# State products and scores in 64x64 tiles of TensorE, one PSUM bank of outputs per head, low parts of nine pairs by GpSimd

## The chip, the cores and the metric

The kernel runs on one core of a Trainium2 chip. The metric is the device time of one execution in microseconds (us), and the median of three runs before the change is 563.88 us (563.80 to 564.11). The core has five engines that each work through a list of instructions in order: TensorE (PE, matmuls, with its weight loads shown as PEld), VectorE (DVE), ScalarE (ACT), GpSimd (POOL), and SyncE (SP), which issues the DMAs. They wait for one another on semaphores.

## The reference

Four batches, eight heads of width 64 and 768 positions go through a linear attention with decay, in blocks of 64, and its output is the input of a mixer with two dense layers over positions and two over channels:

```python
for b in range(nb):                     # blocks of 64 positions
    intra = (qb @ kb.T * Dmask) @ vb    # Dmask[i,j] = lam**(i-j) for i >= j
    inter = (qb * lam**(pos+1)) @ kv_state
    out[:, :, sl] = intra + inter
    kv_state = lam**block * kv_state + (kb * lam**(block-1-pos)).T @ vb
x = out as (batch, 768, 512)
u = x + (relu(x.T @ w_tok1) @ w_tok2).T
result = u + relu(u @ w_ch1) @ w_ch2
```

All of it is in fp32.

## The kernel before, in words

The sixteen pairs of heads (batch b, two heads of 64 each) are the unit of the attention. Blocks of 128 positions are used, so a pair has six blocks c = 0 to 5. Head h of a pair lies in partitions h*64 to h*64+63 of the transposed q and k (`qT`, `kT`).

The main loop (L641 to L725) is written out by hand: the order in which the code calls the engines is the order of each engine's list. I call its pass with index i "turn i". Turn i makes the scores of pair i+1, the outputs of pair i and the state products of pair i+1, turns (transposes) q and k of pair i+2, issues the loads of v of pair i+3 and of q and k of pair i+4, and turns the outputs of pair i back. Beside that it takes `work`, up to five groups of the mixer's token layers (`token_hidden`, 18 matmuls of 256 columns; `token_out`, 6 matmuls of 384 columns) from a queue; turns 0 to 3 have none, turns 4, 5, 6, 11 and 12 have two, turns 7 and 10 five, 8, 9 and 13 four, 14 three and 15 one. `cuts` says how many groups stand ahead of the first `turn_back`, between the two and behind the second. `later` hands out pieces of the conversion of the weights (the `narrow` steps, mostly on DVE, and `split`, on ACT and POOL) between them.

What a turn does for the attention:

- `scores` (L290): for each of two halves g of three blocks, and each head, one matmul of K = 64 rows, M = 128 weight columns, N = 128 (shown as tile 64*128), each head in a PSUM bank of its own; then DVE multiplies by the decay mask into `a` (L307).
- `scale_q` (L249): POOL multiplies q by the powers of lam into `qs` (L252).
- `state` (L258): ten matmuls (tile 128*64, N = 64) make the state contributions `kv` in a bank, a scan on DVE (L273) sums them over the blocks into `sv`, and `place` copies them on POOL (L286) to `stb`, a block-diagonal 128x128 matrix for each block: head h's 64x64 state in the rows and columns of head h, zeros elsewhere. Two `stb` buffers are cleared at the start (L189).
- `outputs` (L315), twice: for three blocks each, two matmuls of the weights `a` with v (L323, K = 128, M = 64) and two of `stb` with `qs` (L333, K = 128, of which half the rows are zeros) into one bank `xT`, head h in partitions h*64 on; then ACT copies the bank to `uT` (L340).
- `turn_q` (L223): q of pair i+2 from pair 5 on, and k from pair 8 on, are loaded in pieces such that DVE's 32x32 transposes finish the turn (L226, L229); the earlier pairs are turned by PE through PSUM (`turn_k` L216, `turn_q_rows` L236) and copied by ACT.
- `turn_back` (L344), twice: PE turns three blocks of `uT` into a bank `xp` (L355), ACT rounds them to `xhi` (L363) and DVE makes the low parts `xlo` = xp - xhi (L364). Both feed `token_hidden`.

An fp32 matmul shows as two MATMUL records in the trace, a transpose or one in fp32r (the mixer's) as one.

PSUM has eight banks: four for `sc` (two buffers of two banks), one named `xT`, and three that rotate under the tag `sh`, which serve `kv`, the second output half, `kt`, `qt`, `xp` and the mixer's groups in the order of the calls. A tile of `sh` waits until the tile three places before it has been read.

After turn 15 the remaining token layers and the sixteen units of the channel layers follow (about two thirds of the time); the change does not touch their code.

Of the kernel before, what the change touches and what calls it, by code (L numbers as in the profile page):

```python
# [22 lines left out]
def kernel(  # L23
# [199 lines left out]
    def turn_q(i):  # L223
        qTs[i] = kp.tile([P, S], F32, tag="qT", bufs=2, name=f"qT{i}")
        if i >= NQ:
            nc.vector.transpose(out=qTs[i], in_=loaded[i][1])  # L226
        if i >= NKD:
            kTs[i] = kp.tile([P, S], F32, tag="kT", bufs=2, name=f"kT{i}")
            nc.vector.transpose(out=kTs[i], in_=krs[i])  # L229
# [28 lines left out]
    def state(i):  # L258
# [22 lines left out]
        st = stb[i % 2]  # L281

        def place():
            for h in range(2):
                r = slice(h * D, (h + 1) * D)
                nc.gpsimd.tensor_copy(out=st[r, :, h, :], in_=sv[r].rearrange("p (e c) -> p c e", c=NC - 1))  # L286

        return place

    def scores(i):  # L290
        b, p = pairs[i]
        for g in range(2):
            pair = two_banks(f"sc{i}{g}", 3 * P)
            sc = [pair[:, h] for h in range(2)]
            for c in range(3):
                cs = slice((3 * g + c) * P, (3 * g + c + 1) * P)
                for h in range(2):
                    r = slice(h * D, (h + 1) * D)
                    nc.tensor.matmul(  # L299
                        out=sc[h][:, c * P : (c + 1) * P],  # L300
                        lhsT=kTs[i][r, cs],
                        rhs=qTs[i][r, cs],
                        start=True,
                        stop=True,
                    )
# [9 lines left out]
    def outputs(i, g):  # L315
        b, p = pairs[i]
        st = stb[i % 2]
        xT = bank("sh" if g else "xT", f"xT{i}{g}", 3 * P)
        for cg in range(3):
            c = 3 * g + cg  # L320
            cs = slice(cg * P, (cg + 1) * P)
            for h in range(2):
                nc.tensor.matmul(  # L323
                    out=xT[h * D : (h + 1) * D, cs],
                    lhsT=vns[i][:, h, c, :],
                    rhs=weights_of[i, g, h][:, cg, :],
                    start=(cg == 0),
                    stop=False,
                )
            if c == 0:  # L330
                continue
            for h in range(2):
                nc.tensor.matmul(  # L333
                    out=xT[h * D : (h + 1) * D, cs],
                    lhsT=st[:, c - 1, h, :],
                    rhs=qss[i][:, c - 1, :],
                    start=False,
                    stop=(cg == 2),
                )
        nc.scalar.copy(out=uT[b][:, p, 3 * g * P : (3 * g + 3) * P], in_=xT)  # L340
# [300 lines left out]
    for i in range(-2, NI):  # L641
# [668 lines left out]
```

## Time and profile before

| What | us |
|---|---|
| runs (median, lowest, highest) | 563.88, 563.80, 564.11 |
| the profiled execution | 563.57 |
| its span, first to last instruction | 561.6 |
| around the span | 2.0 |
| PE busy in the span | 544.1 |
| DVE busy | 433.4 |
| POOL busy | 271.6 |
| ACT busy | 244.2 |
| scores of pair 1 begin (turn 0) | 13.86 |
| scores of pair 8 begin (turn 7) | 75.70 |
| scores of pair 15 begin (turn 14) | 151.35 |
| outputs of pair 15 end (turn 15) | about 166 |
| one group of `token_hidden` on PE (turn 14, 160.06 to 162.18) | 2.1 |
| one group of `token_out` on PE (turn 15, 163.42 to 164.67, with two changes of tile shape) | 1.2 |

The first group of numbers is of the whole execution, the rest of the stage that the change touches. A turn lasts 6.6 to 7.5 us without groups of the mixer and 9.7 to 12.4 us with them.

### The profile page before, as it was taken

What the parts mean: (1) busy time and instruction counts of PE and PEld (TensorE: products, weight loads), DVE (VectorE), ACT (ScalarE), POOL (GpSimd) and SP (SyncE); (2) the same over time, 40 slices, a digit from 0 to 9 for tenths busy, and PEclk for the clock granted to TensorE, in tenths of its full rate; (3) what the DMA queues carried; (4) which work ended last, traced back from release to release, by engine and by line L of the source; (5) the groups of instructions that cost most, each with busy time, mean ns of one, the idle gap of its engine ahead of it and who ended that gap; (6) DMA issues with size and microseconds to landing.
All of it is one profiled execution on the core that took longest, in us unless ns stands there. A gap on an engine that the chain in (4) does not pass through costs nothing.

```text
span 561.6 us, 10781 instructions
## 1 busy us (share of the span) xinstructions
PE 544.1 (97%) x4186; PEld 529.2 (94%) x4186; DVE 433.4 (77%) x650; ACT 244.2 (43%) x490; POOL 271.6 (48%) x248
## 2 busy tenths in 40 slices
PE   5999998999999999999999999999999999999994
PEld 4888887999999999999999999999999999999994
DVE  4786789598787989887878887888678777785683
ACT  3564442336253554343444344353455545442421
POOL 5666452557214464443444454453466656662330
PEclk9999999999999999999999999999999999999998
DMA  9998999999102433351725300015864131320337
GB/s 185 253 205 198 211 166 182 188 190 155 28 2 82 176 119 131 104 215 40 246 73 210 109 1 1 0 29 75 212 113 136 57 114 57 113 76 0 45 49 133
DMA packets 176019, 65.72 MB, mean 117 GB/s; under 512 B 163552, under 2 KB 166752, under 8 KB 175968
## 3 DMA queue, kind: packets, MB, share of 16 engines
q1 hardware_dynamic: 172224, 63.75, 47.8%
q10 hardware_dynamic: 3744, 1.28, 0.9%
q8 instruction: 33, 0.54, 0.4%
q14 instruction: 18, 0.15, 0.1%
HBM read 48.24 MB, written 16.78 MB: 116 GB/s over the span
## 4 chain that ended last, share of the span: by engine, by line
PE 82%; DVE 6%; SPq 5%; DMA 4%; ACT 1%; issue 1%; DVEq 0%; ACTq 0%
PE po L1007 23%; PE pa L794 12%; PE pc L794 9%; PE pb L794 7%; PE pa L981 6%; PE pc L981 5%; PE ph L451 4%; PE pd L794 3%; SPq L111 3%; PE sc L299 2%; PE xT L323 2%; DMA vn<-in_v_dram 2%; PE pu L488 2%; PE pu L471 1%; PE xT L333 1%
## 5 line engine op out<-in xcount | busy, mean ns | idle before, releaser
L1022 DVE TENSOR_TENSOR uT<-po,uT 128x768 f32<-128x768 f32 x62 | 58.9, 952 | 22.6 <-PE po L1007 22.3
L286 POOL COPY stb<-sv 64x320 f32<-64x320 f32 x32 | 26.8, 838 | 45.0 <-DVE sv L273 44.1
L805 ACT ACTIVATE c<-c 128x384 f32<-128x384 f32 x42 | 22.1, 526 | 59.2 <-DVE c L850 33.4
L987 DVE TENSOR_TENSOR uT<-pa,uT 128x768 f32<-128x768 f32 x32 | 30.6, 956 | 11.0 <-PE pa L981 10.3
L323 PE MATMUL xT<-a,vn 128*64 128x128 f32 x384 | 35.7, 277 | 0.0
L340 ACT COPY uT<-xT 128x384 f32<-128x384 f32 x32 | 15.3, 478 | 46.2 <-PE xT L333 46.2
L807 POOL TENSOR_TENSOR h22l<-c,h22h 128x384 fp32r<-128x384 f32 x14 | 14.4, 1030 | 41.6 <-ACT h22h L806 41.6
L307 DVE TENSOR_TENSOR a<-sc,mask 128x768 f32<-128x768 f32 x32 | 29.0, 948 | 5.1 <-PE sc L299 5.1
L333 PE MATMUL xT<-qs,stb 128*64 128x128 f32 x320 | 31.3, 273 | 0.0
L987 DVE TENSOR_TENSOR uT<-pc,uT 128x768 f32<-128x768 f32 x24 | 22.9, 955 | 10.6 <-PE pc L981 10.6
L375 POOL TENSOR_TENSOR c1l<-cs,c1h 128x512 fp32r<-128x512 f32 x15 | 19.2, 1292 | 23.2 <-ACT c1h L374 23.2
L451 PE MATMUL ph<-xhi,w1h 128*128 128x256 f32 x96 | 28.2, 294 | 1.3 <-DVE sv L273 0.9
L1007 PE MATMUL po<-h12h,c 128*128 128x384 f32 x112 | 28.7, 337 | 0.0
L1007 PE MATMUL po<-h11h,c 128*128 128x384 f32 x112 | 28.6, 336 | 0.0
L1007 PE MATMUL po<-h21h,c 128*128 128x384 f32 x112 | 28.6, 336 | 0.0
L1007 PE MATMUL po<-h22h,c 128*128 128x384 f32 x112 | 28.6, 336 | 0.0
L451 PE MATMUL ph<-xhi,w1l 128*128 128x256 f32 x96 | 27.1, 282 | 0.0
L451 PE MATMUL ph<-xlo,w1h 128*128 128x256 f32 x96 | 27.1, 282 | 0.0
L299 PE MATMUL sc<-qT,kT 64*128 64x128 f32 x384 | 26.4, 285 | 0.2 <-ACT qT L237 0.2
L299 PEld LDWEIGHTS sc<-qT,kT 64*128 64x128 f32 x384 | 23.4, 192 | 3.3 <-issue 1.8
L364 DVE TENSOR_TENSOR xlo<-xp,xhi 128x384 fp32r<-128x384 f32 x32 | 17.6, 552 | 11.2 <-ACT xhi L363 11.0
L252 POOL TENSOR_TENSOR qs<-qT,lamp 128x640 f32<-128x640 f32 x16 | 25.2, 1577 | 0.3
(401 smaller groups left out, 1928.8 us busy)
## 6 DMA issues: line engine op xcount, KB each, us to landing
raw<-in_moe_w_ch_dram SPq DMA_DIRECT2D x20, 512.0 KB, 3.8
vn<-in_v_dram SPq DMA_DIRECT2D x16, 384.0 KB, 5.2
kn<-in_k_dram SPq DMA_DIRECT2D x30, 192.0 KB, 5.4
out_dram<-y SPq DMA_DIRECT2D x96, 48.0 KB, 1.9
qn<-in_q_dram SPq DMA_DIRECT2D x44, 96.0 KB, 3.9
kr<-in_k_dram SPq DMA_DIRECT2D x32, 96.0 KB, 2.8
dc1h<-c1h SPq DMA_DIRECT2D x4, 768.0 KB, 5.4
dc1l<-c1l SPq DMA_DIRECT2D x4, 768.0 KB, 6.8
```

The source lines that it names most:

```text
L252: nc.gpsimd.tensor_mul(out=qss[i], in0=qTs[i][:, P:].rearrange("p (c i) -> p c i", i=P), in1=lamp[:, p, None, :].broadcast_to([P, NC - 1, P]),
L286: nc.gpsimd.tensor_copy(out=st[r, :, h, :], in_=sv[r].rearrange("p (e c) -> p c e", c=NC - 1))
L299: nc.tensor.matmul(out=sc[h][:, c * P : (c + 1) * P], lhsT=kTs[i][r, cs], rhs=qTs[i][r, cs], start=True, stop=True,)
L307: nc.vector.tensor_mul(out=a, in0=pair.rearrange("p h (c i) -> p h c i", i=P), in1=mask[:, 2 * p : 2 * p + 2, None, :].broadcast_to([P, 2, ...
L323: nc.tensor.matmul(out=xT[h * D : (h + 1) * D, cs], lhsT=vns[i][:, h, c, :], rhs=weights_of[i, g, h][:, cg, :], start=(cg == 0), stop=False,)
L333: nc.tensor.matmul(out=xT[h * D : (h + 1) * D, cs], lhsT=st[:, c - 1, h, :], rhs=qss[i][:, c - 1, :], start=False, stop=(cg == 2),)
L451: nc.tensor.matmul(out=ph, lhsT=w[:, c, fs], rhs=x[:, c], start=(i == 0), stop=(i == 3 * NC - 1))
L794: nc.tensor.matmul(out=to, lhsT=w[:, t], rhs=x[:, t], start=(start and i == 0), stop=(i == 5), skip_group_check=not start,)
L981: nc.tensor.matmul(out=pair[x][:, t], lhsT=w[:, t], rhs=h, start=(start and i == 0), stop=(i == 2), skip_group_check=not start,)
L987: nc.vector.tensor_add(out=ub, in0=pair[x], in1=ub)
L1007: nc.tensor.matmul(out=to, lhsT=w[:, jj, t * P : (t + 1) * P], rhs=h, start=(i == 0), stop=(i == 3 * JG - 1))
L1022: nc.vector.tensor_add(out=ub, in0=po, in1=ub)
```

## The change

- `outputs` no longer works by halves of blocks but by heads. `from_states` first makes the state products of all blocks c = 1 to 5 and both heads: 64x64 states as weights (K = 64 rows of head h, M = 64), output partitions by the parity of c, a PSUM bank for each head. Then `outputs(i, 0)` and `outputs(i, 1)` add the products of `a` with v for one head each, with the column half of the array chosen by the parity of c instead of by the head. Each bank is copied to `uT` by two ACT copies of 64 partitions. Head 0's bank is one of `sh`, head 1's the bank `xT`.
- In a turn both `outputs` now stand ahead of `state`, and in turn 15 the group that stood between the two halves goes behind them.
- `state` needs no block diagonal: `place` is one POOL copy of 128 partitions, and the two clears of `stb` are gone.
- `scores` splits each matmul into two with 64 weight columns each.
- For pairs 5 to 13 ACT copies `xp` to SBUF (`xf`), rounds from there to `xhi`, and POOL makes the low part; the other pairs stay with DVE.
- The k transposes of DVE are a step of their own (`turn_k_dims`), called behind the first part of the turn's groups.
- `cuts` puts at least one group ahead of the first `turn_back` where the turn has any.

```diff
-    stb = []
-    for i in range(2):
-        st = ap.tile([P, NC - 1, 2, D], F32, name=f"stb{i}")
-        nc.gpsimd.memset(st, 0.0)
-        stb.append(st)
+    states = {}
...
+
+    def turn_k_dims(i):
         if i >= NKD:
             kTs[i] = kp.tile([P, S], F32, tag="kT", bufs=2, name=f"kT{i}")
             nc.vector.transpose(out=kTs[i], in_=krs[i])
...
-        def place():
-            for h in range(2):
-                r = slice(h * D, (h + 1) * D)
-                nc.gpsimd.tensor_copy(out=st[r, :, h, :], in_=sv[r].rearrange("p (e c) -> p c e", c=NC - 1))
-
-        return place
+        states[i] = st = ap.tile([P, NC - 1, D], F32, tag="st", bufs=2, name=f"st{i}")
+        return lambda: nc.gpsimd.tensor_copy(out=st, in_=sv.rearrange("p (e c) -> p c e", c=NC - 1))
...
-                    nc.tensor.matmul(
-                        out=sc[h][:, c * P : (c + 1) * P],
-                        lhsT=kTs[i][r, cs],
-                        rhs=qTs[i][r, cs],
-                        start=True,
-                        stop=True,
-                    )
+                    for half in range(2):
+                        js = slice(half * D, (half + 1) * D)
+                        nc.tensor.matmul(
+                            out=sc[h][js, c * P : (c + 1) * P],
+                            lhsT=kTs[i][r, cs][:, js],
+                            rhs=qTs[i][r, cs],
+                            start=(c == 0),
+                            stop=(c == 2),
+                            skip_group_check=True,
+                        )
...
-    def outputs(i, g):
+    xTs = {}
+
+    def from_states(i):
+
+        xTs[i] = [bank(t, f"xT{i}{h}", 3 * P) for h, t in enumerate(("sh", "xT"))]
+        for n in range(3):
+            for c in (2 * n, 2 * n + 1):
+                if c == 0:
+                    continue
+                for h in range(2):
+                    r = slice(h * D, (h + 1) * D)
+                    nc.tensor.matmul(
+                        out=xTs[i][h][c % 2 * D : (c % 2 + 1) * D, n * P : (n + 1) * P],
+                        lhsT=states[i][r, c - 1, :],
+                        rhs=qss[i][r, c - 1, :],
+                        start=(c in (1, 2)),
+                        stop=False,
+                        skip_group_check=True,
+                    )
+
+    def outputs(i, h):
         b, p = pairs[i]
...
+        for n in range(3):
+            for c in (2 * n, 2 * n + 1):
                 nc.tensor.matmul(
-                    out=xT[h * D : (h + 1) * D, cs],
+                    out=xTs[i][h][c % 2 * D : (c % 2 + 1) * D, n * P : (n + 1) * P],
                     lhsT=vns[i][:, h, c, :],
-                    rhs=weights_of[i, g, h][:, cg, :],
...
-            for h in range(2):
-                nc.tensor.matmul(
-                    out=xT[h * D : (h + 1) * D, cs],
-                    lhsT=st[:, c - 1, h, :],
-                    rhs=qss[i][:, c - 1, :],
-                    start=False,
-                    stop=(cg == 2),
-                )
-        nc.scalar.copy(out=uT[b][:, p, 3 * g * P : (3 * g + 3) * P], in_=xT)
+        u = uT[b][h * D : (h + 1) * D, p].rearrange("d (n m i) -> d m n i", m=2, i=P)
+        for m in range(2):
+            src = xTs[i][h][m * D : (m + 1) * D].rearrange("d (n i) -> d n i", i=P)
+            nc.scalar.copy(out=u[:, m], in_=src)
...
+        if NQ <= i < NI - 2:
+            xf = ap.tile([P, 3, P], F32, tag="xf", bufs=2, name=f"xf{i}{g}")
+            nc.scalar.copy(out=xf, in_=src)
+            nc.scalar.copy(out=hi, in_=xf)
+            nc.gpsimd.tensor_sub(out=lo, in0=xf, in1=hi.bitcast(F32))
+        else:
+            nc.scalar.copy(out=hi, in_=src)
+            nc.vector.tensor_sub(out=lo, in0=src, in1=hi.bitcast(F32))
...
         if i >= 0:
+            from_states(i)
             outputs(i, 0)
+            outputs(i, 1)
         place = state(i + 1) if 0 <= i + 1 < NI else None
         work = [groups.popleft() for _ in range(take.get(i, 0))]
-        if i == NI - 1:
-            work.pop(0)()
-        if i >= 0:
-            outputs(i, 1)
...
-        n = early.get(i, len(work) // 4)
+        n = early.get(i, max(min(1, len(work)), len(work) // 4))
...
+            if n == 0 and i + 2 < NI:
+                turn_k_dims(i + 2)
```

How the order of the instructions moves is shown at three places. The first is PE in turn 10 (scores `sc` of pair 11, outputs `xT` of pair 10, state contributions `kv` of pair 11); a row's shape is that of the output, and a row counts fp32 matmuls once. Before:

```order
L299 MATMUL sc_1743<-qT_1657,kT_1659 128x128 x6
L299 MATMUL sc_1752<-qT_1657,kT_1659 128x128 x6
L323 MATMUL xT_1763<-a_1605,vn_1431 64x128 x4
L333 MATMUL xT_1763<-qs_1616,stb_119 64x128 x2
L323 MATMUL xT_1763<-a_1605,vn_1431 64x128 x2
L333 MATMUL xT_1763<-qs_1616,stb_119 64x128 x2
L265 MATMUL kv_1775<-vn_1583,kd_1683 64x64 x10
L323 MATMUL xT_1788<-a_1614,vn_1431 64x128 x2
L333 MATMUL xT_1788<-qs_1616,stb_119 64x128 x2
```

The same place of the changed kernel, where the two banks of outputs are `xT_1798` (head 0) and `xT_1799` (head 1), from the second half of the scores to the state contributions:

```order
L293 MATMUL sc_1781<-qT_1670,kT_1700 64x128 x12
L321 MATMUL xT_1798<-qs_1626,st_1669 64x128
L321 MATMUL xT_1799<-qs_1626,st_1669 64x128
L321 MATMUL xT_1798<-qs_1626,st_1669 64x128
L321 MATMUL xT_1799<-qs_1626,st_1669 64x128
L321 MATMUL xT_1798<-qs_1626,st_1669 64x128
L321 MATMUL xT_1799<-qs_1626,st_1669 64x128
```

Four more rows of state products follow there, then twelve products of `a` with v, six for each head, and only then the ten of `kv`. So all state products stand directly behind the scores, and `kv` has moved behind the whole of the outputs.

The second place is DVE in turn 7: `sv` is the scan, L226 and L229 (later L222 and L227) are the transposes of q and k of pair 9, L493 (L504) reads a mixer group from PSUM, and the rows on `uT_63` are narrowing of weights. Before:

```order
L273 SCALAR_TENSOR_TENSOR sv_1200<-keep,kv_1189 128x320
L226 STREAM_TRANSPOSE qT_1216<-qn_989 128x768
L229 STREAM_TRANSPOSE kT_1218<-kr_996 128x768
L493 TENSOR_TENSOR uT_60<-pu_1224,uT_60 128x384
L383 TENSOR_SCALAR uT_63<-uT_63 128x512
L364 TENSOR_TENSOR xlo_1074<-xp_1233,xhi_1073 128x3x128
L386 SCALAR_TENSOR_TENSOR uT_63<-uT_63 128x512
L493 TENSOR_TENSOR uT_60<-pu_1243,uT_60 128x384
```

And of the changed kernel:

```order
L271 SCALAR_TENSOR_TENSOR sv_1340<-keep,kv_1329 128x320
L222 STREAM_TRANSPOSE qT_1343<-qn_1085 128x768
L504 TENSOR_TENSOR uT_60<-pu_1349,uT_60 128x384
L227 STREAM_TRANSPOSE kT_1358<-kr_1092 128x768
L394 TENSOR_SCALAR uT_63<-uT_63 128x512
L504 TENSOR_TENSOR uT_60<-pu_1372,uT_60 128x384
L397 SCALAR_TENSOR_TENSOR uT_63<-uT_63 128x512
L504 TENSOR_TENSOR uT_60<-pu_1381,uT_60 128x384
```

The k transpose has moved behind the reading of the first group, and the `xlo` row has left DVE.

The third place is POOL in turns 7 and 8 (`qs` are the scaled q, `stb` and `st` the placed states, `w2l` the low part of a weight). Before:

```order
L252 TENSOR_TENSOR qs_1175<-qT_1066,lamp 128x640
L286 COPY stb_117<-sv_1200 64x5x64 x2
L252 TENSOR_TENSOR qs_1316<-qT_1216,lamp 128x640
L286 COPY stb_119<-sv_1341 64x5x64 x2
L252 TENSOR_TENSOR qs_1464<-qT_1357,lamp 128x640
```

And of the changed kernel:

```order
L250 TENSOR_TENSOR qs_1299<-qT_1177,lamp 128x640
L280 COPY st_1342<-sv_1340 128x320
L386 TENSOR_TENSOR w2l<-uT_63,w2h 128x512
L372 TENSOR_TENSOR xlo_1210<-xf_1364,xhi_1209 128x3x128
L372 TENSOR_TENSOR xlo_1210<-xf_1403,xhi_1209 128x3x128
L250 TENSOR_TENSOR qs_1460<-qT_1343,lamp 128x640
L280 COPY st_1503<-sv_1501 128x320
```

Two low parts now stand between the placing of one pair's state and the scaling of the next pair's q, and the placing is one copy where it was two; the row of `w2l` stood ahead of `qs` of that turn before.

More of the change, by code (lines that the diff above doesn't have):

```diff
@@ L280, in state @@
         )
-        st = stb[i % 2]
-        def place():
-            for h in range(2):
-                r = slice(h * D, (h + 1) * D)
-                nc.gpsimd.tensor_copy(out=st[r, :, h, :], in_=sv[r].rearrange("p (e c) -> p c e", c=NC - 1))
-        return place
+        states[i] = st = ap.tile([P, NC - 1, D], F32, tag="st", bufs=2, name=f"st{i}")
+        return lambda: nc.gpsimd.tensor_copy(out=st, in_=sv.rearrange("p (e c) -> p c e", c=NC - 1))
     def scores(i):
@@ L313, in scores @@
                 weights_of[i, g, h] = a[:, h]
-    def outputs(i, g):
-        b, p = pairs[i]
[L317 to L321, printed above, removed]
-            for h in range(2):
+    xTs = {}
[15 more added lines that the diff above has]
+                    )
@@ L323, in outputs @@
+    def outputs(i, h):
+        b, p = pairs[i]
+        for n in range(3):
+            for c in (2 * n, 2 * n + 1):
                 nc.tensor.matmul(
-                    out=xT[h * D : (h + 1) * D, cs],
+                    out=xTs[i][h][c % 2 * D : (c % 2 + 1) * D, n * P : (n + 1) * P],
                     lhsT=vns[i][:, h, c, :],
-                    rhs=weights_of[i, g, h][:, cg, :],
-                    start=(cg == 0),
-                    stop=False,
-                )
-            if c == 0:
-                continue
@@ L332, in outputs @@
-            for h in range(2):
-                nc.tensor.matmul(
-                    out=xT[h * D : (h + 1) * D, cs],
-                    lhsT=st[:, c - 1, h, :],
-                    rhs=qss[i][:, c - 1, :],
-                    start=False,
-                    stop=(cg == 2),
-                )
-        nc.scalar.copy(out=uT[b][:, p, 3 * g * P : (3 * g + 3) * P], in_=xT)
+                    rhs=weights_of[i, c // 3, h][:, c % 3, :],
+                    start=False,
+                    stop=(n == 2),
@@ L342 @@
+                    skip_group_check=True,
+                )
+        u = uT[b][h * D : (h + 1) * D, p].rearrange("d (n m i) -> d m n i", m=2, i=P)
+        for m in range(2):
+            src = xTs[i][h][m * D : (m + 1) * D].rearrange("d (n i) -> d n i", i=P)
+            nc.scalar.copy(out=u[:, m], in_=src)
     x_of = {}
@@ L362, in turn_back @@
         src = xp.rearrange("p (c e) -> p c e", e=P)
-        nc.scalar.copy(out=hi, in_=src)
-        nc.vector.tensor_sub(out=lo, in0=src, in1=hi.bitcast(F32))
+        if NQ <= i < NI - 2:
[6 more added lines that the diff above has]
+            nc.vector.tensor_sub(out=lo, in0=src, in1=hi.bitcast(F32))
     w1h = tokp.tile([P, NC, FT], F32R, name="w1h")
```

## The prediction

> **What bounds the kernel now.** I read the page first: engines, the DMA digits, the chain.
>
> ```profile
> span 561.6 us, 10781 instructions
> PE 544.1 (97%) x4186; PEld 529.2 (94%) x4186; DVE 433.4 (77%) x650; ACT 244.2 (43%) x490; POOL 271.6 (48%) x248
> DMA  9998999999102433351725300015864131320337
> PE 82%; DVE 6%; SPq 5%; DMA 4%; ACT 1%; issue 1%; DVEq 0%; ACTq 0%
> ```
>
> PE is busy for 97% of the span and holds 82% of the chain that ended last, so time taken from PE's list comes off the end unless a wait takes its place. The DMA digits warn: in the ten slices up to 140 us, the stage of the change, the DMA engines are at nine tenths or more too. The stretches of turns 0 to 2 with a part of 3, of turn 7, and of turns 10 and 12 say more (PE, PEld, DVE, ACT, POOL busy, clock, DMA share, GB/s):
>
> ```profile
> 20.00:42.00 22.00, 21.45 (x319) 18.72 (x318) 18.55 (x27) 13.63 (x31) 14.61 (x13) 1.00 1.06 220
> 75.70:88.10 12.40, 11.53 (x125) 10.10 (x124) 12.37 (x21) 4.31 (x9) 5.97 (x5) 1.00 0.94 177
> 111.00:121.75 10.75, 10.75 (x126) 10.13 (x125) 9.52 (x16) 5.08 (x11) 6.18 (x7) 1.00 0.95 182
> 131.85:141.60 9.75, 9.75 (x131) 9.35 (x130) 7.85 (x13) 4.16 (x9) 5.92 (x5) 1.00 0.99 177
> ```
>
> Late turns are PE alone (10.75 of 10.75); in turn 7 DVE is full (12.37 of 12.40) and PE idles for 0.9; early the DMAs are full (1.06). So a microsecond less of PE work is worth all of it late, less early.
>
> **State products.** PE's list in turn 10, by start and length:
>
> ```profile
> 110.99 1.61 PE L299 MATMUL sc<-qT,kT 64*128 64x128 f32 x24
> 112.53 0.66 PE L323 MATMUL xT<-a,vn 128*64 128x128 f32 x8
> 113.02 0.39 PE L333 MATMUL xT<-qs,stb 128*64 128x128 f32 x4
> 113.24 0.39 PE L323 MATMUL xT<-a,vn 128*64 128x128 f32 x4
> 113.46 0.39 PE L333 MATMUL xT<-qs,stb 128*64 128x128 f32 x4
> 113.67 0.75 PE L265 MATMUL kv<-vn,kd 128*64 128x64 f32 x20
> 114.25 0.39 PE L323 MATMUL xT<-a,vn 128*64 128x128 f32 x4
> ```
>
> What a row costs is the distance to the next start. Four records with 128 columns (two heads, two passes each) take 0.22 (113.02 to 113.24), 55 ns a record; twenty with 64 columns take 0.58 (113.67 to 114.25), 29 ns a record. Half the columns, half the time: the two column tiles of a head pair run beside each other, and no record needs more than 29 ns to be issued. The state products of a pair are five rows of 0.22, 1.09. In 64x64 tiles the records stay twenty, but four can run at once: block 1 alone, then 2 with 3, 4 with 5, three rows of 0.22, 0.66. Bounds: 20 x 29 ns = 0.58 if only issue counts, and 1.09 if still only two run at once. I take 0.66, because two tiles already show no loss. **16 x 0.43 = 6.9 less.**
>
> **Scores.** They become 48 records in place of 24. Now they take 1.54 with the change of tile shape behind them (110.99 to 112.53); 24 x 55 ns are 1.3 of it. Four at once: 48 x 29 ns = 1.4, or 12 x 0.11 = 1.3. Two at once: 48 x 55 ns = 2.6. I take no difference; bounds are 1 less and 2 more over sixteen pairs while four run, 21 more if two. The products with v stay 24 records in two column tiles. The number of changes of tile shape in a turn stays at three, since scores and state products now share one.
>
> The Trainium skill (TensorE: Matmul & The Clock Gate, Part 3: Packing small matmuls — row/col tiling) says that a weight load overlaps running matmuls only if it goes to another row group, which the two halves of a split score tile do not. By it the sum would be that of two at once, below. The trace does not agree: the 128*64 tiles share all rows and run at 55 ns a record with a weight load for each.
>
> **Waits of PE that go, move and come.** PE's weight loads, 15 to 175 us, by what they waited for (sum, times, longest):
>
> ```profile
> PEld kt L216 <- DVE sv L273: 1.8, 3, 1.0
> PEld ph L451 <- DVE sv L273: 1.2, 1, 1.2
> PEld pu L488 <- DVE uT L493: 0.9, 2, 0.5
> PEld xp L355 <- DVE uT L493: 0.8, 1, 0.8
> PEld xp L355 <- DVE xlo L364: 0.8, 1, 0.8
> PEld ph L451 <- DVE uT L493: 0.5, 1, 0.5
> PEld ph L451 <- DVE xlo L364: 0.5, 2, 0.3
> ```
>
> These 6.5 us are banks of `sh` that DVE had not yet read. The 1.2 goes: in turn 6 the bank of `kv` was needed by the group third behind it, and now a whole group of 18 matmuls (2.1 us) lies between. The 1.3 on `xlo` goes, since the bank of `xp` is then read by ACT alone. Of the 2.2 on `uT` I count half, 1.1: turn 7 is full of DVE work, from which two low parts leave and ahead of whose first group the k transpose no longer stands. **3.6 less** (bounds 0 and 6.5).
>
> The 1.8 does not go but grows. `kv` now follows all outputs, so its bank is wanted six transposes behind its end in turns 0 to 5, where outputs lay between before. Six of them take 0.7 (34.11 to 34.79), and the scan comes only after the mask products:
>
> ```profile
> 34.11 0.85 PE L236 MATMUL qt<-ident,qn 128*128 128x128 f32 x6
> 34.79 1.01 PE L355 MATMUL xp<-ident,uT 128*128 128x128 f32 x6
> ...
> 45.79 1.81 DVE L307 TENSOR_TENSOR a<-sc,mask 128x768 f32<-128x768 f32 x2
> 47.52 0.81 DVE L273 TENSOR_TENSOR_SCAN sv<-keep,kv 128x320 f32<-128x320 f32 x1
> ```
>
> At least 0.2 + 0.81 lie between the end of `kv` and the bank, 0.3 more than 0.7, and up to 1 where DVE is behind, as here: six turns of 0.5 are 3.0 in place of 1.8. **1.2 more** (0 to 3).
>
> **ACT, POOL and the copies.** Durations (columns: busy, mean ns of one; for L807 minimum, median, maximum):
>
> ```profile
> L340 ACT COPY uT<-xT 128x384 f32<-128x384 f32 x32 | 15.3, 478 | 46.2 <-PE xT L333 46.2
> L363 ACT CAST xhi<-xp 128x384 fp32r<-128x384 f32 x32 | 15.3, 479 | 8.7 <-PE xp L355 8.7
> L364 DVE TENSOR_TENSOR xlo<-xp,xhi 128x384 fp32r<-128x384 f32 x32 | 17.6, 552 | 11.2 <-ACT xhi L363 11.0
> L286 POOL COPY stb<-sv 64x320 f32<-64x320 f32 x32 | 26.8, 838 | 45.0 <-DVE sv L273 44.1
> L807 POOL TENSOR_TENSOR h22l<-c,h22h x14: 1012/1016/1191, 189.3 to 391.2; 128x384 fp32r<-128x384 f32 x14
> ```
>
> ACT gets 32 more copies at 0.48 (15.3) and 18 `xf` at 0.48 (8.6), on an engine busy for under half. The last two copies of a pair end about 1.2 behind its last output; PE has `kv` (0.58) and a group (at least 1.0) or transposes (0.7) in that time, and only without that cover would each of the 16 turns lose up to 1. DVE loses 18 x 0.552 = 9.9. POOL loses 16 copies of 0.84 (13.4) and gets 18 low parts at 1.02 (18.3); these wait for ACT's two steps, and behind them in POOL's list stand `qs` and `st`, wanted a turn later, so 5 us in nine turns hide. The moved k transpose now holds back the second group's read (0.93); the group takes longer. I take 0 for all of this, bounds 0 and 2 more.
>
> POOL has a price for DVE, however:
>
> ```profile
> 61.38 0.68 DVE L386 SCALAR_TENSOR_TENSOR uT<-uT,uT 128x512 uint32<-128x512 uint32 x1
> 83.95 1.59 DVE L386 SCALAR_TENSOR_TENSOR uT<-uT 128x512 uint32<-128x512 uint32 x1
> 83.36 1.63 POOL L252 TENSOR_TENSOR qs<-qT,lamp 128x640 f32<-128x640 f32 x1
> ```
>
> The same step takes 0.68 alone and 1.59 while POOL's product runs. In turns 7 and 8, where narrowing runs on a full DVE, I charge a blocking each less the copy that goes: **0.5 more** (0 to 2). The Trainium skill (SBUF — State Buffer, SBUF: two separate sides) has this as a rule: a VectorE instruction with two SBUF inputs and a GpSimd one that reads SBUF take one port pair in turn. The trace agrees (0.91 longer). By the rule alone every low part could block one such step, 18 x 0.9 = 16 of DVE and more than the 9.9 that leave; then the waits would stay.
>
> **Early turns belong to the DMAs.** The last q of pair 4 and who needs it:
>
> ```profile
> 28.63 1.69 SPq L136 DMA_DIRECT2D qn<-in_q_dram  x2
> qn<-in_q_dram SPq DMA_DIRECT2D x8, 192.0 KB, 4.5
> ```
>
> The second of two issues starts near 29.5 and lands 4.5 later, at 34.0; PE takes it at 34.11 (row above). A faster turn 2 would only wait there, so the 0.43 of turns 0 to 2 is not had: **1.3 more** (0 to 1.3). Later there is slack:
>
> ```profile
> 135.46 3.35 SPq L111 DMA_DIRECT2D kr<-in_k_dram  x4
> kr<-in_k_dram SPq DMA_DIRECT2D x32, 96.0 KB, 2.8
> 146.78 0.93 DVE L229 STREAM_TRANSPOSE kT<-kr 128x768 f32<-128x768 f32 x1
> ```
>
> The last piece of k starts by 138.3, lands near 141 and is turned at 146.78: 5.7 us, plus the first group by which the turn moves back.
>
> **Sum.** -6.9 - 3.6 + 1.2 + 0.5 + 1.3 = -7.5. Against the profiled execution, 563.57 (span 561.6 and 2.0 around it, 0.3 under the median of 563.88), that is 556.1, and 556.4 by the median. I say **556.3**. With the bounds: best 6.9 + 1.3 (issue alone) + about 3 of the other waits, 552; worst of this case 561.
>
> **Rivals.**
>
> *Two tiles at once, not four* (slower). Place: PE's array in `scores` and `from_states`. Price: 48 x 55 ns, 1.3 more a pair, 21 in all, state products no shorter; with some 3 of the waits gone about 581. It decides at the point where a record costs 38 ns: then scores rise by the 0.5 a pair that all else brings. For it: no row shows four at once, and 29 ns is as fast as any record goes. Against: tiles pair without loss both by rows (`sc`) and by columns (`xT`, `kv`).
>
> *The loads pace the stage.* SP issues without pause and the DMA share is 0.94 to 1.06. If the loads keep their pace, each turn past a shift of about 5 waits on k: 559.5 to 560.5. Against: the moved k transpose, and buffers that come free earlier.
>
> *The waits stay* (the low parts do not do what they are moved for): DVE, blocked by POOL or late with the scan, holds the banks as before. -6.9 + 1.2 + 1.3 + 0.5 is -3.9: 559.7. For it: the two rows of L386. Against: DVE still loses 9.9.
>
> *Everything given back*: copies and scan late in each turn, 0.45 a turn: about 563.5.
>
> **How the numbers follow.** Forecast 0.66 (552 to 559), loads 0.09, waits 0.10, given back 0.04, two tiles 0.11. Faster by over 0.2% (1.1 us, about what a measurement of this kernel can tell from no change): 0.85; within it 0.03; slower 0.12. The range 552 to 561 takes in forecast, loads and waits and leaves out some 0.17.
>
> **What would show it.** State products: 20 records from the end of the scores in about 0.66, not 1.09. Scores: 48 records in about 1.5, not 2.8; the latter makes the prediction wrong at once. No wait of `xp` or `ph` on `xlo` in turns 5 to 13. New waits on `sv` of about 0.5 in turns 0 to 5. The scores of pair 3 hardly earlier than before, those of pair 15 some 7 us earlier, and the mixer behind it of the same length. Any wait on kr, or on POOL's `xlo`, `qs` or `st`, speaks for the rivals.

## The result and the profile after

The changed kernel takes 568.12 us (median of 7 runs, 566.25 to 571.48) beside 563.88 before (563.43 to 565.28 on the same chip): ratio 1.0079, interval 1.0049 to 1.0108. It is **slower by 4.2 us** where 7.5 less were forecast. Its profiled execution is the slowest of the seven (571.48, span 569.7); the spread comes back further down. The page:

```profile
span 569.7 us, 11597 instructions
PE 541.5 (95%) x4570; PEld 525.8 (92%) x4570; DVE 429.2 (75%) x632; ACT 268.8 (47%) x540; POOL 276.9 (49%) x248
PEclk9999978999999999999999999999999999999998
PE 80%; DMA 6%; DVE 6%; ACT 3%; SPq 2%; issue 1%; POOL 1%; ACTq 0%; DVEq 0%
```

PE is busy for 2.6 us less although the span is 8.1 longer, so PE waits more; and the granted clock dips in the sixth and seventh slices (71 to 100 us), which the page of before doesn't show. The tiles themselves do what was said. PE's timeline in turn 9:

```profile
106.17 1.54 PE L293 MATMUL sc<-qT,kT 64*64 64x128 f32 x48
107.54 0.83 PE L321 MATMUL xT<-qs,st 64*64 64x128 f32 x20
108.30 1.53 PE L334 MATMUL xT<-a,vn 128*64 128x128 f32 x24
109.66 0.75 PE L263 MATMUL kv<-vn,kd 128*64 128x64 f32 x20
110.34 0.39 PE L462 MATMUL ph<-xhi,w1h 128*128 128x256 f32 x1
```

From the scores to the first group behind the pair's work are 4.17 us (106.17 to 110.34), where they were 4.68 (110.99 to 115.67). That is 0.51 a pair, **8.2 in all**: 48 score records take 1.37, so four tiles do run at once.

Where it is lost, by the distance between the starts of the scores of successive pairs (PE timelines; the third kernel is experiment e10 below):

| turn | before | after | e10 |
|---|---|---|---|
| 1 | 7.35 | 8.21 | 7.38 |
| 4 | 11.54 | 11.31 | 11.27 |
| 5 | 10.61 | 11.73 | 11.22 |
| 6 | 11.27 | 14.81 | 10.51 |
| 7 | 12.43 | 14.58 | 11.73 |
| 8 | 12.05 | 11.18 | 12.48 |
| 9 | 10.81 | 10.30 | 10.30 |
| 10 | 10.75 | 11.83 | 10.68 |
| 11 | 10.10 | 11.31 | 10.12 |
| scores of pair 15 begin | 151.35 | 158.73 | 149.80 |
| span behind that | 410.27 | 410.97 | 410.77 |

Turn 9 keeps its 0.51; turns 6 and 7 lose 5.7 and turns 1, 5, 10 and 11 another 4.3. Not all of that is the change's: e9, e12 and e13 below have the same code up to turn 5, and take 7.23 to 7.56 in turn 1 and 10.89 in turn 5. The longest waits of PE's weight loads in the same stretch as in the prediction (15 to 182 in this longer kernel; sum, times, longest; rows of `issue`, which name no tile, are left out):

```profile
PEld ph L462 <- ACT xf L370: 2.7, 3, 1.3
PEld xp L360 <- DVE sv L271: 2.2, 1, 2.2
PEld xp L360 <- ACT uT L345: 1.8, 3, 0.7
PEld sc L293 <- DVE kT L227: 1.6, 1, 1.6
PEld ph L462 <- DVE h L467: 1.4, 1, 1.4
PEld pu L499 <- POOL w2l L386: 1.3, 1, 1.3
PEld qt L234 <- DVE sv L271: 1.2, 2, 0.8
```

Every part of the change has a wait here that wasn't there or was shorter: `xf` and `w2l` (the low parts' new way and what is queued with it), `sv` and `uT` (products behind all outputs, four copies), `kT` (k turned late). I added up, for turns 0 to 14, every start of a PE row that came over 0.18 later than such a row usually does: 6.0 us before, 17.9 after. The clock adds the rest. Windows of after (columns as in the prediction; the clock is the third number from the end):

```profile
74.00:75.00 1.00, 0.50 (x3) 0.38 (x3) 1.00 (x2) 0.00 (x0) 0.49 (x1) 0.84 0.98 157
75.00:81.00 6.00, 5.00 (x32) 4.50 (x34) 4.67 (x8) 4.26 (x9) 3.83 (x5) 0.50 1.08 224
81.00:82.00 1.00, 1.00 (x36) 1.00 (x32) 1.00 (x2) 0.00 (x0) 1.00 (x1) 0.75 1.11 194
88.00:89.00 1.00, 0.80 (x3) 0.73 (x4) 0.17 (x1) 0.67 (x1) 0.15 (x1) 0.66 0.61 93
89.00:91.00 2.00, 2.00 (x9) 2.00 (x8) 1.59 (x3) 1.50 (x4) 0.43 (x1) 0.50 1.06 320
91.00:92.00 1.00, 1.00 (x6) 1.00 (x5) 0.61 (x2) 0.41 (x1) 0.58 (x1) 0.63 1.00 198
```

PE runs at half its clock twice, behind its two longest idle stretches. Half of what it was busy there, about 4.5 us, is lost. So the account of the profiled execution is -8.2 (tiles) + 11.9 (waits) + 4.5 (clock) = +8.2, measured +8.1. The count of late starts depends on what is called usual, so that it meets the measured number within 0.1 is luck.

How turn 6, which begins at 65.60, comes to its wait, on DVE and on POOL (some rows of each):

```profile
64.28 1.39 DVE L403 SCALAR_TENSOR_TENSOR uT<-uT 128x512 uint32<-128x512 uint32 x1
68.57 0.42 DVE L467 SCALAR_TENSOR_TENSOR hl<-ph,hh 128x256 fp32r<-128x256 f32 x1 [2.57 <-ACT hh L466]
68.91 1.35 DVE L397 SCALAR_TENSOR_TENSOR uT<-uT,uT 128x512 uint32<-128x512 uint32 x1
70.19 1.80 DVE L400 TENSOR_SCALAR uT<-uT 128x512 f32<-128x512 f32 x1
71.91 1.81 DVE L302 TENSOR_TENSOR a<-sc,mask 128x768 f32<-128x768 f32 x2
73.64 0.81 DVE L271 TENSOR_TENSOR_SCAN sv<-keep,kv 128x320 f32<-128x320 f32 x1
```

```profile
63.84 1.28 POOL L372 TENSOR_TENSOR xlo<-xf,xhi 128x384 fp32r<-128x384 f32 x1 [3.93 <-ACT xhi L371]
68.71 1.00 POOL L372 TENSOR_TENSOR xlo<-xf,xhi 128x384 fp32r<-128x384 f32 x1
69.68 2.02 POOL L250 TENSOR_TENSOR qs<-qT,lamp 128x640 f32<-128x640 f32 x1
```

The first low part of pair 5 runs beside a narrowing step of DVE and stretches it to 1.39 (0.69 in e14 below, which has no low part there). ACT's list waits for that step and has the new copies `xf` in it, so its `hh` is late, and DVE stands idle for 2.57. Then a low part and `qs`, which it held back, run beside two more narrowing steps and stretch them (0.68 and 0.42 alone). The mask products and the scan queue behind, and PE waits for the scan's bank until 74.50. Counted from the start of the turn, the scan is 3.4 later than in e14: 1.3 by the late `hh`, 2.1 by the two steps.

### The profile page after: what moved, and what is told of

It reads as the page before. It is cut to its first block, busy times and chain, and to the rows that moved or that the text cites. A ratio compares the mean times of both kernels' runs of the same rounds, so it can differ in the third digit from the quotient of the medians.

```text
span 569.7 us, 11597 instructions
## 1 busy us (share of the span) xinstructions
PE 541.5 (95%) x4570; PEld 525.8 (92%) x4570; DVE 429.2 (75%) x632; ACT 268.8 (47%) x540; POOL 276.9 (49%) x248
## 4 chain that ended last, share of the span: by engine, by line
PE 80%; DMA 6%; DVE 6%; ACT 3%; SPq 2%; issue 1%; POOL 1%; ACTq 0%; DVEq 0%
PE po L1018 23%; PE pa L805 12%; PE pc L805 9%; PE pb L805 7%; PE pa L992 6%; PE pc L992 4%; DMA qn<-in_q_dram 4%; PE ph L462 3%; PE pu L499 3%; PE pd L805 3%; PE sc L293 2%; PE xT L334 2%; PE pu L482 1%; DMA uT<-in_moe_w_tok_dram 1%; SPq L111 1%
## 5 line engine op out<-in xcount | busy, mean ns | idle before, releaser
L345 ACT COPY uT<-xT 64x384 f32<-64x384 f32 x64 | 30.3, 473 | 24.2 <-PE xT L334 23.2
L280 POOL COPY st<-sv 128x320 f32<-128x320 f32 x16 | 13.7, 857 | 33.8 <-DVE sv L271 33.8
L372 POOL TENSOR_TENSOR xlo<-xf,xhi 128x384 fp32r<-128x384 f32 x18 | 19.6, 1093 | 18.2 <-ACT xhi L371 18.2
L293 PE MATMUL sc<-qT,kT 64*64 64x128 f32 x768 | 25.8, 281 | 1.6 <-DVE kT L227 1.4
L293 PEld LDWEIGHTS sc<-qT,kT 64*64 64x64 f32 x768 | 21.9, 139 | 4.9 <-issue 1.9
L462 PEld LDWEIGHTS ph<-xhi,w1h 128*128 128x128 f32 x96 | 19.1, 199 | 6.1 <-ACT xf L370 2.7
L334 PE MATMUL xT<-a,vn 128*64 128x128 f32 x384 | 24.5, 277 | 0.0
```

Of the source, the lines that this page charges most:

```text
L293: nc.tensor.matmul(out=sc[h][js, c * P : (c + 1) * P], lhsT=kTs[i][r, cs][:, js], rhs=qTs[i][r, cs], start=(c == 0), stop=(c == 2), skip_g ...
L334: nc.tensor.matmul(out=xTs[i][h][c % 2 * D : (c % 2 + 1) * D, n * P : (n + 1) * P], lhsT=vns[i][:, h, c, :], rhs=weights_of[i, c // 3, h][ ...
L345: nc.scalar.copy(out=u[:, m], in_=src)
L462: nc.tensor.matmul(out=ph, lhsT=w[:, c, fs], rhs=x[:, c], start=(i == 0), stop=(i == 3 * NC - 1))
```

## Experiments: the parts alone

A turn is called a pass in the expectations. Theory 1 blames the low parts on GpSimd, theory 2 the place of the state products, theory 3 that of the k transpose; theory 4 (the group cuts), 5 (loads) and 6 (the clock) came up on the way. All ratios are to the kernel before, on the same chip.

**e1**, the low parts back on DVE:

```diff
-        if NQ <= i < NI - 2:
+        if False:
```

> The changed kernel, but the low parts of pairs 5 to 13 are again taken by VectorE straight from PSUM; no copy xf. Theory 1 (the low parts on GpSimd cost the time: they stand in POOL's list ahead of qs and the low parts of the weights, block VectorE's narrowing, and ACT waits for an xf buffer): the waits that name xf, xhi, w2l and the late scan of turn 6 go, 2.7 + 1.3 + about 3.5, and some 2 of slow matmuls behind them; 560 to 562. Theory 2 (the place of the state products behind all outputs costs it): the scan stays late, 566 to 568. Theory 3 (the k transpose behind the first group costs it): no change, 567 to 568.

Measured 566.74, ratio 1.0052 (1.0034 to 1.0070). Turn 6 falls from 14.81 to 9.85, but turn 8 rises from 11.18 to 14.33: DVE, full again, is late there with the low parts that left it. The longest wait there (2.2, of `xp` on `xlo`) stands behind a narrowing step that `qs` stretched to 1.94 and behind the k transpose. A gain of 1.4, not 6 to 8, and within the uncertainty of the two medians. The time falls in theory 2's branch, but not in theory 2's way, since turn 6 is cured.

**e2**, `state(i + 1)` between `outputs(i, 0)` and `outputs(i, 1)`:

> The changed kernel, but the state products of the next pair stand between the outputs of the two heads, so that their scan can start some 0.9 us earlier in each turn. Theory 1: 566 to 568. Theory 2: the waits kt, qt, ph and xp on sv in turns 0 to 6 (1.2 + 1.1 + 1.2 + 2.2, about 5 with the others behind the scan) go, less two more changes of tile shape a turn (0.1 to 0.2 each, 16 turns: 2 to 4); 562 to 566. Theory 3: 567 to 568, or slower by the changes of shape.

Measured 566.45, 1.0049 (1.0028 to 1.0070): 1.7 less, which the intervals don't separate from nothing either. Turn 6 stays at 14.47.

**e3**, `turn_k_dims(i + 2)` right behind `turn_q(i + 2)`:

> The changed kernel, but k is again turned by VectorE right behind q, ahead of the first group. Theories 1 and 2: only the wait of the scores on kT in turn 13 goes (1.6): 566 to 567. Theory 3: the turns that end with a transposed k late (turns 7 to 13) gain 0.5 each: 563 to 564.5.

Measured 567.68, 1.0066 (1.0054 to 1.0078). Turn 11 falls from 11.31 to 9.87 as a k wait of 1.4 goes; the rest stays, and the median differs by less than it is uncertain.

**e4**, all three at once and the cuts as before, which leaves the tiles and banks:

```diff
-        n = early.get(i, max(min(1, len(work)), len(work) // 4))
+        n = early.get(i, len(work) // 4)
```

> The changed kernel with the tiles and banks alone: low parts by VectorE, state products between the outputs of the heads, k turned behind q, groups cut as before. If the tiles are worth what their rows show (0.5 a pair) and theories 1, 2 and 3 hold the loss between them: 556 to 560. If the tiles' gain is taken back by the loads, or by the copies of outputs (four a pair in place of two, in strips of 64 rows), 562 to 566.

Measured 564.92, 1.0019 (1.0011 to 1.0028): the worse branch. Four turns lose their gain again, as here turn 12:

```profile
136.89 0.33 PE L360 MATMUL xp<-ident,uT 128*128 128x128 f32 x1 [0.57 <-ACT uT L345]
137.39 0.33 PE L360 MATMUL xp<-ident,uT 128*128 128x128 f32 x1 [0.17 <-ACT uT L345]
```

Against the usual distance these two are 0.73 and 0.39 late, 1.12 in all, because ACT's four copies of the outputs end behind them and no group covers them. The others are turns 6, 11 and 14.

**e5** is e4 with the new cuts; **e6** is e5 with the state products behind all outputs; **e8** is e5 with all low parts on GpSimd:

> The tiles and banks alone, but with the groups cut as in the change (at least one group ahead of the first transposes back). In the kernel with the tiles alone PE waited 1.12 in passes 6, 11, 12 and 14 for ACT's copies of the outputs, which end some 1.1 behind the last output and nothing of PE's lay between. Theory 1a (the copies of outputs without cover took the tiles' gain): these four waits go and the time falls from 564.9 to 559.5 to 561. Theory 5 (loads and VectorE's narrowing set the pace whatever PE does): the wait moves on to passes 7 and 8, and 563.5 to 565 remains.

> As e5_tiles_new_cuts, but the state products stand behind the outputs of both heads as in the change; so this one and the other tell the price of that place alone. Theory 2 (a late scan makes everything late that stands behind it on VectorE, and st on GpSimd, with the low parts of w2 behind it): 2 to 5 slower than the other, nearly all of it in passes 7 and 8. Against theory 2: equal or up to 2 faster, since the state products then cover the copies of the outputs and save two changes of tile shape a pass.

> As e5_tiles_new_cuts, but all low parts of pairs 5 to 13 by GpSimd as in the change; so this one and the other tell their price where the rest is as before. Theory 1: 3 to 5 slower than the other, most of it in pass 6 (two narrowing steps of VectorE at three times their length, and the scan behind them) and 1 in pass 10. If the low parts cost only together with the late state products: within 1.5 of the other.

| kernel | median | ratio (interval) | against e5 |
|---|---|---|---|
| e5 | 564.79 | 1.0009 (0.9993 to 1.0025) | |
| e6 | 565.83 | 1.0031 (1.0019 to 1.0043) | +1.0 |
| e8 | 569.16 | 1.0074 (1.0058 to 1.0091) | +4.4 |

The place of the products costs about 1, less than theory 2 wanted, and the intervals of e5 and e6 overlap. The low parts cost 4.4 by the medians and 3.7 by the ratios, clear of the intervals: theory 1, where the state products and k stand as they did before. Most of it is turn 6, which goes from 10.51 to 15.65. In e5 the uncovered copies are gone (turns 5, 6: 10.48 and 10.51), but turn 7 takes 14.46. The time is that of theory 5's branch; the next run shows that its cause is another.

## Experiments: one conversion step, one place too late

POOL in turn 7 of e5, and then what PE waited for there:

```profile
79.86 0.78 POOL L280 COPY st<-sv 128x320 f32<-128x320 f32 x1 [4.80 <-DVE sv L271]
80.59 1.27 POOL L386 TENSOR_TENSOR w2l<-uT,w2h 128x512 fp32r<-128x512 f32 x1
```

```profile
80.18 0.45 PE L499 MATMUL pu<-w2h,hh 128*128 128x384 f32 x1 [0.99 <-ACT w2h L385]
81.92 0.44 PE L499 MATMUL pu<-w2l,hh 128*128 128x384 f32 x1 [1.12 <-POOL w2l L386]
```

The last split of `w2` stands behind `st` on POOL and behind the output copies on ACT; before, and in e4, it stood ahead of them. The new cuts did this: `later` gives out one step more while over five are waiting, and with calls in another order the list came out one step behind. **e10** is e5 with one step more:

```diff
+        if i == 6:
+            later(1)
         if i == -1:
             load_w1(0)
```

> As e5_tiles_new_cuts (which has 564.8 and spreads over 5), but one more step of the weight conversion is issued at the end of pass 6, so that the last split of w2 stands ahead of pass 7's copies on ACT and of st on GpSimd, as it does in the kernel before and in the one with the tiles alone. Theory 4 (the new cuts reorder the list of conversion steps by one, and that step is what pass 7 waits for): the waits of pu in pass 7 (1.2 and 1.3) and the half clock behind them go, pass 7 falls from 14.5 to about 12, the time to 561 to 563. Rival (VectorE's narrowing sets the pace in passes 7 and 8): pass 8 gives it back, 564 to 565.

Measured **561.36, 0.9961 (0.9948 to 0.9975)**: 3.4 less than e5 by the medians, 2.7 by the ratios, and faster than the kernel before. POOL in turn 7:

```profile
77.98 1.29 POOL L386 TENSOR_TENSOR w2l<-uT,w2h 128x512 fp32r<-128x512 f32 x1 [3.43 <-ACT w2h L385]
79.23 1.56 POOL L250 TENSOR_TENSOR qs<-qT,lamp 128x640 f32<-128x640 f32 x1
80.73 0.80 POOL L280 COPY st<-sv 128x320 f32<-128x320 f32 x1
```

**e12** is the changed kernel with that step alone:

> The changed kernel with nothing else than that one step of the conversion issued earlier. Theory 4: in pass 7 the waits of pu (0.9 and 1.2) and the second stretch of half clock (88 to 92) go, 2.5 to 4 in all: 564 to 565.5. Theory 1 alone (the low parts on GpSimd make the conversion late wherever its last step is issued): 567 to 568.

Measured 566.72, 1.0047 (1.0034 to 1.0059): 1.4 less, between the two branches and within the uncertainty of the medians. Turn 7 falls from 14.58 to 11.94 and its half clock is gone, but turn 6 keeps 14.72; the median gained less than the profiled execution since most runs of the change were not as slow as that one. Undone one at a time, the parts give 1.4 (e1), 1.7 (e2), 0.4 (e3) and 1.4 (e12); between the change and e10, where all four are undone, lie 6.8. So what one of them costs depends on the others.

## Experiments: what a long wait costs

**e9** and **e13** give PE useless work where the change waits:

```diff
+            if i == 6 and n == 0:
+                fill = bank("xT", "fill", 3 * P)
+                for x in range(14):
+                    nc.tensor.transpose(..., in_=uT[0][:, 0, 0:P], identity=ident)
             if n < 2 and i >= 0:
                 turn_back(i, n)
```

> The changed kernel plus 14 transposes of TensorE into a spare bank that nobody reads, ahead of the first group of pass 6: 1.6 us of useless work on PE's list, where PE waits 2.2 for the scan soon after. Theory 6 (a PE idle for about 2 us gets half the clock for some 4 us, so that long waits cost twice): the 2.2 become about 0.6, the granted clock stays at 1.00 from 74 to 78, pass 6 falls from 14.8 to 12 to 13, and the time by 1.5 to 3, to 565 to 566.5, though PE does more work. Against theory 6: the useless work lies in the wait and the time stays at 567.5 to 569, or it adds its 1.6.

e9 missed its aim: 568.32, 1.0082 (1.0070 to 1.0094). Its bank, one of `sc`, was itself held by the late mask products, so the filling waited 2.9 and only moved the wait. e13 (the diff above, on e12) uses a bank that is free:

> As e12_change_split_earlier (566.7, pass 6 of 14.7 with waits of 2.1 and 1.4 and half the clock from 74 to 80.5) plus 14 useless transposes, 1.6 us of PE, behind the first group of pass 6, into the bank of the copied outputs, which is free by then. Theory 6 (a long idle stretch halves the clock): the first wait falls to about 0.5, the clock stays at 1.00 at least until the second, pass 6 falls to 12 to 13, the time to 564 to 565.5 with more work. Against it: 566.5 to 568.

Measured **564.46, 1.0016 (1.0006 to 1.0026): 2.3 less than e12 by the medians (1.7 by the ratios) with 1.6 more work on PE.** Turn 6 fell only to 13.96, not to 12 to 13. The two kernels, e12 first, by windows:

```profile
73.00:75.00 2.00, 0.59 (x4) 0.36 (x4) 2.00 (x5) 0.40 (x1) 0.76 (x1) 0.76 1.06 168
75.00:79.09 4.09, 4.09 (x18) 3.87 (x19) 3.29 (x4) 3.48 (x8) 2.99 (x3) 0.50 1.02 233
```

```profile
73.00:75.00 2.00, 0.91 (x7) 0.43 (x5) 2.00 (x3) 0.00 (x0) 0.76 (x1) 1.00 1.03 164
75.00:78.89 3.89, 3.37 (x19) 3.15 (x19) 3.86 (x6) 3.66 (x8) 2.52 (x2) 0.70 0.95 211
```

The wait of 1.90 for the scan became 0.38, and half of the half clock went with it; the second wait (1.23, on DVE's `h`) still stands ahead of the other half. Two kernels put a wait alone into turn 9 of e10, by useless scans on DVE and a transpose that needs them:

> As e10_split_one_step_earlier (561.4), plus one useless scan on VectorE (0.8) behind the scan of pass 9 and one transpose on PE that waits for it: a PE wait of about 1.1 in a pass that had none. Theory 6: no half clock, pass 9 from 10.3 to 11.4, 562 to 562.8. Against theory 6: the same.

> As e15_wait_short with three useless scans, so a PE wait of about 2.7. Theory 6: half the clock for about 4 us behind it, so that pass 9 or 10 pays some 1.9 on top of the wait: 565 to 566.5. Against theory 6 (a wait costs its length): 563.5 to 564.3.

The waits came out longer than meant, since DVE's list held more behind the scan:

```profile
107.04 0.45 PE L689 MATMUL fill<-ident,slow 128*128 128x128 f32 x1 [3.07 <-DVE slow L680]
```

```profile
110.47 0.45 PE L689 MATMUL fill<-ident,slow 128*128 128x128 f32 x1 [6.00 <-DVE slow L680]
```

566.31, 1.0045 (1.0028 to 1.0063), and 570.46, 1.0114 (1.0099 to 1.0128). Turn 9 grew from 10.30 to 16.11 and 18.44: 5.8 for a wait of 3.1 and 8.1 for one of 6.0. So a long wait costs its length and some 2 to 2.7 more, at both lengths. The clock can account for that: it is at half for 6.82 in both (106.04 to 112.86 and 108.14 to 114.96), PE works in 5.8 and 4.5 of it, and half of these is 2.9 and 2.2. That is theory 6, at other lengths than the expectations had, and so at other times; the wait of 1.1 was not tried alone.

## Experiments: where low parts cost, and the tiles apart

**e14** is e12 with `8 <= i` in place of `NQ <= i`; **e7**, **e11** and **e17** move low parts in e5, e10 and e10 with `i in (8, 9)`, the same, and `i == 8`:

> As e12_change_split_earlier, but the low parts of pairs 5, 6 and 7 by VectorE again; those of pairs 8 to 13 stay on GpSimd. Theory 1 with its place (they cost where the weights of the first mixer step are narrowed, by blocking VectorE and by standing ahead of qs): pass 6 falls from 14.7 to 10.5 and no stretch of half clock is left there, 562 to 563.5. If they cost everywhere alike: a third of the 1.4 to 4.4 that undoing all of them gave, 565 to 566.5.

> As e5_tiles_new_cuts, but the low parts of pairs 8 and 9 alone by GpSimd: there VectorE is full and PE waited for it (1.2 and 0.4 in pass 8), and GpSimd had long idle times. Theory 1 as a matter of place (the low parts cost where the weights are converted in passes 5 to 7, and gain where VectorE is full): 0.5 to 1.5 faster than e5_tiles_new_cuts. If every low part on GpSimd costs: slower by 0.5 to 2.

> As e10_split_one_step_earlier, with the low parts of pairs 8 and 9 by GpSimd (which took 1.6 off e5_tiles_new_cuts). If both gains add: 559.5 to 561.5, faster than the kernel before by 0.5 to 0.8%. If the narrowing of pass 6 meets GpSimd's qs as it did in that run: 562 to 563.

> As e10_split_one_step_earlier (561.4), with the low parts of pair 8 alone by GpSimd. In e11_best_try those of pairs 8 and 9 took 0.85 off pass 8 and put 0.5 on pass 10. If the gain and the cost belong to the one and the other pair: 560 to 561. If the runs of half clock that come and go decide: 561 to 562.5, as before.

| kernel | median | ratio (interval) |
|---|---|---|
| e14 | 564.01 | 0.9998 (0.9988 to 1.0008) |
| e7 | 563.14 | 0.9983 (0.9969 to 0.9997) |
| e11 | 562.26 | 0.9972 (0.9958 to 0.9986) |
| e17 | 561.44 | 0.9956 (0.9943 to 0.9970) |

e14 is 2.7 below e12, somewhat less than expected: turn 6 falls from 14.72 to 9.86 while turns 8 and 10 stay (11.13, 11.79) and turn 7 rises from 11.94 to 12.59. Its DVE shows the two steps of turn 6 with their usual length, and the scan 3.4 earlier than in the change, counted from the start of the turn (64.38 here, 65.60 there):

```profile
66.36 0.68 DVE L397 SCALAR_TENSOR_TENSOR uT<-uT,uT 128x512 uint32<-128x512 uint32 x1
66.96 0.42 DVE L400 TENSOR_SCALAR uT<-uT 128x512 f32<-128x512 f32 x1
67.29 1.81 DVE L302 TENSOR_TENSOR a<-sc,mask 128x768 f32<-128x768 f32 x2
69.03 0.81 DVE L271 TENSOR_TENSOR_SCAN sv<-keep,kv 128x320 f32<-128x320 f32 x1
```

So most of what the low parts cost comes from pairs 5 to 7. Those of pair 8 help turn 8 (e10 12.48, e17 11.63) and those of pair 9 put 0.5 on turn 10 (e11 11.18, e17 10.67), but e17's runs, 559.97 to 563.0, have the same median as e10's: what it gains isn't shown beyond the spread. e10 and e17 are the best versions, about 2.6 faster than the kernel before.

**e18** is e10 with the scores in 64x128 tiles again:

> As e10_split_one_step_earlier, but the scores again in 64x128 tiles, 24 a pair; the state products stay in 64x64 tiles. If four tiles at once cost and bring the scores nothing (the prediction's term): one more change of tile shape a pass, 561.4 to 562.5. If the scores' tiles bring what the rows show beside one another (1.53 to 1.37 a pair, 0.16): up to 2.5 more on PE's list, 562 to 563.5 where no wait takes it in.

Measured 565.00, 1.0013 (1.0003 to 1.0024): above both branches, 3.6 more than e10 by the medians and 2.9 by the ratios. Turns 9 to 13 are each 0.19 to 0.23 longer than in e10 (10.30 to 10.53 in turn 9), so the scores' tiles, with the change of tile shape that they save, are worth 0.2 a pair, some 3.5 of PE's list in all, and the state products the rest of the 0.51. (A stretch of half clock in its turn 6, 75 to 78, is not counted there.)

## Why the prediction was wrong

- **State products: right.** 0.66 a pair was said, 0.76 to the next kind of row was measured, with the change of tile shape in it.
- **Scores: mechanism right, size off.** The term was nothing; it measured 0.2 a pair (e18), with the saved change of tile shape in it. "Two tiles at once" is out: 48 records take 1.37, not 2.6.
- **"3.6 less" of waits: wrong.** "The 1.3 on `xlo` goes": 2.7 on `xf` came in its place, ACT's copy being late, in turn 5 behind a step that waited for the load of `w2`, in turn 8 for one of the two `xf` buffers. "The 1.2 goes" since a group lies between: the group was there, and the scan was 2.2 later than it.
- **"1.2 more" for the late scan: near, but not shown** (1.7 in e2 and 1.0 in e6 against e5, neither clear of its interval, and both for the whole place of the products).
- **The step that failed: "I take 0 for all of this, bounds 0 and 2 more"** on ACT, POOL and the copies, with "0.5 more" for POOL's price in turns 7 and 8. The price per collision was about right (0.9 was said; 0.68 became 1.35, 0.42 became 1.80). The place was wrong: turn 6, where POOL's list held `w2l`, a low part and `qs` close together beside the narrowing. ACT's new copies were priced at nothing too, but a blocked step and the copies `xf` made its `hh` late, and DVE stood idle for 2.57. And the blocked step isn't the whole cost; the mask products, the scan and PE queue behind it. Measured: 4.4 by the medians, 3.7 by the ratios (e8 against e5), most of it from pairs 5 to 7 (e14); within the change, where other parts take it up, 1.4 and not clear of noise (e1).
- **Copies: bound right.** "Only without that cover would each of the 16 turns lose up to 1": e4 shows 1.12 in the turns without a cover, and the new cuts do cover them.
- **The new cuts: a part not seen.** The prediction took them as cover alone. They also moved the last split of `w2` by one place: 3.4 by the medians, 2.7 by the ratios (e10 against e5); 1.4 in the change, not clear of noise (e12).
- **k: wrong.** Its slack was counted from the landing of the load, 5.7. What delayed it is DVE's list, where a narrowing step blocked by POOL stands ahead of it:

```profile
136.46 2.22 DVE L397 SCALAR_TENSOR_TENSOR uT<-uT 128x512 uint32<-128x512 uint32 x1
138.60 0.96 DVE L227 STREAM_TRANSPOSE kT<-kr 128x768 f32<-128x768 f32 x1
```

- **Early turns: about right.** Scores of pair 3 begin at 28.24 before and at 27.70 to 28.42 in e1 to e18, with the state products in either place. The 28.94 of the change's profiled execution is the only later one; its turn 1 is longer than in kernels with the same code there.
- **Not in the sum at all: the clock.** A wait was priced at its length; long ones cost some 2 more, 4.5 in the profiled execution. The spread of the change's runs goes with it: the mean granted clock is 0.988 and 0.989 in the two slowest (571.48, 570.45) and 0.997 in two of the three fastest (566.25, 567.29).

Of the rivals "Everything given back: copies and scan late in each turn" came nearest in time, and had 0.04. Its price was too low, because waits pile up in few turns, where they bring the clock down, and aren't spread as 0.45 over all. "The waits stay" came nearest in mechanism (DVE, blocked by POOL or late with the scan), but let the waits stay as they were, where they grew. "The loads pace the stage" was not put to the test: no wait on `kr` is listed in the change, e10 or e17, but no version comes 5 ahead either (pair 15 of e17 begins at 147.62, 3.7 earlier than before). The load that DVE does wait for is that of `w2`, 2.0 in the change and in e10 and 0.2 in e17; their turn 5 takes 11.73, 11.22 and 10.48. Even e10 does not reach 556.3: no half clock shows in its trace, yet its waits, counted as above, are some 12 where 6.0 were, so some 6 of the 8.2 go into waits, most of them for DVE. That remainder wasn't taken apart by a run.

## What to carry to other kernels

When PE's work shrinks, price each wait that is left by what is queued on the engine it waits for, and not by the one operation added there. An operation moved to GpSimd isn't free because GpSimd has idle time: look at what DVE does in that microsecond, and at what stands behind it in both lists. A rule that hands out background work by counting calls moves that work whenever calls change places.

## What the hardware showed

Half the clock is granted in pieces of one length. From the windows of after: (0.16 + 6 x 0.50 + 0.25) / 0.50 = 6.82 us from 74.68 on, and (0.34 + 2 x 0.50 + 0.37) / 0.50 = 3.42 from 88.32 on: two pieces and one, and the starts lie 13.64, four pieces, apart. The Trainium skill (TensorE: Matmul & The Clock Gate, Part 1: The HAM clock gate) has this as a window of about 3.4 us that runs freely, at half rate after an idle one. The length agrees; but none of these windows was idle throughout. A wait of 2.1 was enough where it lay within one window, and did nothing where it was cut in two. The same wait (2.09, `ph` on DVE's `h`) in turn 6 of e15, PE's row and the window behind it:

```profile
73.19 0.38 PE L463 MATMUL ph<-xhi,w1h 128*128 128x256 f32 x1 [2.09 <-DVE h L468]
```

```profile
74.00:76.00 2.00, 2.00 (x30) 1.87 (x32) 1.45 (x3) 2.00 (x6) 0.84 (x1) 1.00 0.91 128
```

And in turn 6 of e16:

```profile
72.84 0.39 PE L463 MATMUL ph<-xhi,w1h 128*128 128x256 f32 x1 [2.09 <-DVE h L468]
```

```profile
74.00:76.00 2.00, 2.00 (x11) 1.84 (x9) 1.79 (x4) 1.33 (x4) 0.48 (x1) 0.50 1.06 157
```

In e15 a piece begins at 106.04, in e16 at 108.14 (the windows 106 to 107 and 108 to 109 have a clock of 0.52 and 0.57). Ten lengths of 3.41 back lie borders at 71.9 and 74.0. If the borders keep that distance, the one in e15 cuts the wait into 0.8 and 1.3, and the clock stays at 1.00; in e16 the whole wait lies ahead of the border, and the clock falls there. Turn 6 then takes 11.88 in e15 and 12.78 in e16. Two waits of 1.0 and 1.1 close together (turn 7 of e5) also stand ahead of a piece of half clock; single ones of 1.4 (turn 8 of e10) and 1.55 (turn 7 of e14) do not. So the same program can lose time in one run and none in another, by where its waits fall: the runs of e17 go from 559.97 with a mean clock of 0.997 to 563.00 with 0.993.

Four 64x64 tiles run at once though two of them share their rows. The Trainium skill (same page, Part 3: Packing small matmuls — row/col tiling) overlaps weight loads only across row groups; 48 records in 1.37 us, 29 ns each with a weight load for each, do not agree.
